# Mamba-2 scan and squared-ReLU feed-forward: halved first weight tiles, another load order, two small products on VectorE, and other idle products

## The chip, the cores and the metric

The kernel runs on one core of a Trainium2 chip. The metric is the device time of one execution in microseconds (us); lower is better. One execution of the kernel before was also recorded by the hardware profiler; times inside an execution are counted from the start of its span. Engines are called PE (TensorE), DVE (VectorE), ACT (ScalarE), POOL (GpSimd) and SP (SyncE, which here only issues transfers).

## The reference

Two stages follow each other. The first is a chunked state-space scan over x (4 batches, 8 heads, 768 positions, 32 wide), with a decay a per position and B and C (16 wide):

```python
for c in range(nc):                       # chunks along the sequence
    cum = np.cumsum(la, axis=-1)          # la = log(clip(a))
    L = np.exp(cum[..., :, None] - cum[..., None, :]) * causal
    M = np.einsum('bhin,bhjn->bhij', Cc, Bc) * L
    y = np.einsum('bhij,bhjd->bhid', M, xc) \
        + np.einsum('bhin,bhnd->bhid', Cc, state) * np.exp(cum)[..., None]
    state = decay_full[:, :, None, None] * state + np.sum(Bx, axis=2)
```

The second takes the result as 3072 tokens of 256 features:

```python
h = np.maximum(x @ w_in, 0.0)             # w_in 256 x 2048
out = h * h @ w_out                       # w_out 2048 x 256
```

## The kernel before, in words

The work is cut into 12 units of 256 positions: 4 batches times 3 stretches of the sequence, in the order batch first. A unit of the scan goes through these steps:

- loads of C, B and x (`ph_load`, L125; the third unit's x by `load_x`, L142);
- `prep_c`, `prep_b`, `prep_x` (L162 to L191): C times the running decay and B times its inverse are written as bf16 into the tile jt, two instructions each, and x is cast;
- `ph_tr` (L200): jt is transposed, by PE and copies for the first five units and by a transposing transfer for the rest, into bct;
- `ph_mt` (L244): sixteen small products give the raw scores in four PSUM banks; `ph_raw` (L261) copies a bank to SBUF by ACT, and `ph_mask` (L266) applies the causal mask on DVE, from PSUM or from such a copy, into mts;
- `ph_yu` (L273): the products that give the unit's outputs (from mts and from the carried state) and its contribution U to the state; the outputs are cast into the tile T;
- `ph_s` (L346): the new state z, and its bf16 spread S_d = z times QP, computed by POOL (`on_pool`, L366).

The feed-forward part works on T in steps of 256 hidden features, eight per unit: `mm1` (L381) makes four PE products with w_in and one ReLU by ACT into hb; `square` (L393) multiplies hb by itself on DVE into h; `mm2` (L399) makes four PE products with w_out. The weights are loaded by POOL's queue with a cast to bf16, w_in and w_out as four tiles of 512 hidden features each (`load_w_in`, L150, and `load_w_out`, L154).

Everything stands in an order written out by hand: a long opening sequence (L423 to L509) for the first two units, then the string `first`, in which u, s and d with two digits mean mm1, square and mm2 of a unit (first digit) and a step (second digit), and names such as `C2`, `B2`, `tr2` mean the third unit's scan steps; then a loop over the remaining steps. Each engine runs its instructions in this order, and each waits only for what it needs. In the opening sequence PE also runs products on a zero tile, `idle_products` (L157), whose numbers and widths stand in `NIDLE` (L50). POOL's queue carries, in the order of the program text, both POOL's arithmetic and its issues of weight loads, so that a load is issued only after the arithmetic ahead of it:

```python
        first = """
            u00 u01 s00 Y1 d00 s01 u10 z1b d01 u11 C2 s10 u02 s11 u03 d10 inv s02 u12 d11 s03 u13 d02 s12 d03 u04
            s13 d12 u05 B2 s04 d13 free tr2 load3 u14 s05 u15 d04 s14 mt2 d05 m20 s15 U2 m21 d14 m22 prep3 d15 u06 m23
            u16 lend s06 u07 s16 Y2 d06 u17 s07 d16 d07 s17""".split()
```

Of the kernel before, what the change touches and what calls it, by code (L numbers as in the profile page):

```python
# [11 lines left out]
BF16 = mybir.dt.bfloat16  # L12
# [18 lines left out]
def kernel(  # L31
# [13 lines left out]
    nc = tc.nc  # L45
# [1 line left out]
    NU = 12  # L47
    LAG = 4
    NPE = 5
    NIDLE = ((7, 512), (2, 256), (1, 256), (3, 256), (3, 128), (5, 256))  # L50

    const = ctx.enter_context(tc.tile_pool(name="const", bufs=1))
    wpool = ctx.enter_context(tc.tile_pool(name="w", bufs=1))
# [39 lines left out]
    idle = const.tile([128, 128], BF16, name="idle")  # L93


    w_in_b = [wpool.tile([128, 2, 512], BF16, name=f"w_in_b{i}") for i in range(4)]
    w_out_b = [wpool.tile([128, 4, 256], BF16, name=f"w_out_b{i}") for i in range(4)]
    QP = const.tile([128, 12, 2, 4], FP32, name="QP")

    pp = psum.tile([128, 8, 512], FP32, name="pp")  # L100
# [47 lines left out]
        live.setdefault(k, {})["xs"] = xs  # L148

    def load_w_in(i):  # L150
        nc.gpsimd.dma_start(  # L151
            out=w_in_b[i], in_=_dap(moe_w_in, i * 512, [[2048, 128], [128 * 2048, 2], [1, 512]]))

    def load_w_out(i):  # L154
        nc.gpsimd.dma_start(out=w_out_b[i], in_=_dap(moe_w_out, i * 512 * 256, [[1024, 128], [1, 1024]]))

    def idle_products(n, cols):  # L157
        for _ in range(n):
            nc.tensor.matmul(pp[:, 5, 0:cols], idle, _fap(idle, 0, [[0, cols // 128], [1, 128]]),  # L159
                             start=True, stop=True, skip_group_check=True)  # L160
# [39 lines left out]
    def ph_tr(k):  # L200
        v = live.setdefault(k, {})
        bct = big.tile([128, 2, 3, 128], BF16, tag="bct", name=f"bct{k}")
        v["bct"] = bct
        if k >= NPE:
            nc.sync.dma_start_transpose(out=bct.rearrange("p r w t -> p (r w) t"),
                                        in_=jt[k % 3].rearrange("p r w t -> p (r w t)"))
            return
        if k == 0:
            for r in range(2):
                tr = pp[:, 6 + r, 0:192].bitcast(BF16)  # L210
                for w in range(3):
                    nc.tensor.transpose(tr[:, w * 128:(w + 1) * 128], jt[0][:, r, w, :], eye_b)  # L212
                o = bct[:, r].rearrange("p w t -> p (w t)")
                if r == 0:
                    nc.vector.tensor_copy(out=o, in_=tr)
                else:
                    nc.scalar.copy(out=o, in_=tr)
            return
        if k == 1:
            for c, h in ((1, 7), (0, 6)):  # L220
                n = 1 + c
                tr = pp[:, h, 0:128 * n].bitcast(BF16)
                for r in range(2):
                    for w in range(n):
                        o = (r * n + w) * 128
                        nc.tensor.transpose(tr[:, o:o + 128], jt[1][:, r, c + w, :], eye_b)
                nc.scalar.copy(out=_fap(bct, 128 * c, [[384, 2], [1, 128 * n]]), in_=tr)
                if c:
                    idle_products(*NIDLE[4])
            return  # L230
        tr = pp[:, {2: 1, 3: 2}.get(k) or bank(), 0:384].bitcast(BF16)
        for r in range(2):
            for w in range(3):
                o = (r * 3 + w) * 128
                nc.tensor.transpose(tr[:, o:o + 128], jt[k % 3][:, r, w, :], eye_b)  # L235
        o = bct.rearrange("p r w t -> p (r w t)")
        if k == 4:
            nc.scalar.copy(out=o, in_=tr)
        else:
            nc.vector.tensor_copy(out=o, in_=tr)  # L240
# [102 lines left out]
            nc.scalar.copy(out=_fap(T[y], 0, [[64, 2], [128, 4], [1, 64]]),  # L343
                           in_=_fap(pp, h[0] * 512, [[(h[1] - h[0]) * 512, 2], [64, 4], [1, 64]]))

    def ph_s(k, i, later=None, raw=None):  # L346

        b, j = UNITS[k]
        v = live[k]
        if i == 0:  # L350
            v["S"] = [state.get(b, (None, None, None))[2]]
        if j == 2 and i == 1:
            return
        z_old, p_old, _ = state.get(b, (None, None, None))
        h, c = v["U"][i]
        held.discard(h)
        z = spool.tile([128, 64], FP32, tag=f"z{b}", name=f"z{k}_{i}")
        u_in = pp[:, h, c:c + 64] if raw is None else raw
        if z_old is None:
            nc.scalar.copy(out=z, in_=pp[:, h, c:c + 64])  # L360
        else:
            nc.vector.scalar_tensor_tensor(out=z, in0=z_old, scalar=p_old, in1=u_in,  # L362
                                           op0=ALU.mult, op1=ALU.add)
        S_d = spool.tile([128, 256], BF16, tag=f"Sd{b}{i}", name=f"Sd{k}_{i}")

        def on_pool():  # L366
            nc.gpsimd.tensor_tensor(  # L367
                out=_fap(S_d, 0, [[128, 2], [32, 4], [1, 32]]),
                in0=_fap(z, 0, [[32, 2], [0, 4], [1, 32]]),
                in1=_fap(QP, ((b * 3 + j) * 2 + i) * 4, [[0, 2], [1, 4], [0, 32]]), op=ALU.mult)  # L370

        if later is None:
            on_pool()
        else:
            later.append(on_pool)
        state[b] = (z, Ptot[:, i, b * 3 + j:b * 3 + j + 1], S_d)
        v["S"].append(S_d)
# [2 lines left out]

    def mm1(blk, fp, edge):  # L381
        h = bank(edge)
        wb, wo = fp // 2, 2 * (fp % 2)
        for i in range(2):
            for g in range(2):
                nc.tensor.matmul(pp[:, h, i * 256:(i + 1) * 256], _fap(w_in_b[wb], g * 512 + wo + i, [[4, 128]]),  # L386
                                 T[blk][:, g].rearrange("p r u t -> p (r u t)"),
                                 start=(g == 0), stop=(g == 1), skip_group_check=True)
# [9 lines left out]

    def mm2(blk, fp):  # L399
        h2 = h2s.pop((blk, fp))  # L400
        wb, wo = fp // 2, 2 * (fp % 2)
        end = blk == NU - 1
        for r, i in [(r, i) for r in range(2) for i in range(2)] if end else [(r, i) for i in range(2) for r in range(2)]:
            f = 2 * fp + i
            o = pp[:, r, 0:256] if end else pp[:, 7 if blk else 6, r * 256:(r + 1) * 256]
            nc.tensor.matmul(o, h2[:, i, r * 128:(r + 1) * 128], w_out_b[wb][:, wo + i, :],  # L406
                             start=(f == 0 and (end or r == 0)), stop=(f == 15), skip_group_check=True)
        if fp < 7:
            return
# [12 lines left out]
    with tc.manual_schedule():  # L422
# [25 lines left out]
        keep(quad, [[-32, 4]], 0, 1)  # L448
        keep(quad, [[32, 4]], 31, -1)
        idle_products(*NIDLE[0])  # L450
        nc.vector.tensor_scalar(out=a_cl, in0=a_nat, scalar1=1e-6, scalar2=1.0, op0=ALU.max, op1=ALU.min)
        for u in range(2):
            nc.vector.tensor_tensor_scan(out=cp_r[:, u * 128:(u + 1) * 128], data0=a_cl[:, u * 128:(u + 1) * 128],
# [53 lines left out]
        load_w_in(3)  # L507
        load_w_out(3)
        order[:] = [4, 5]  # L509

        def late_states():
# [24 lines left out]
        def scores_only():  # L536
            order[:] = [h for h in order if h > 3]

        phases = {
            "z1b": lambda: (ph_s(1, 1, later=later), ph_s(0, 1, later=later, raw=U01)), "Y1": second_outputs, "C2": lambda: prep_c(2, nc.gpsimd), "free": scores_only,  # L540
            "inv": lambda: nc.vector.reciprocal(out=_fap(Pinv, 1, [[96, 2], [3, 32], [1, 2]]),
                                                in_=_fap(P_sb, 1, [[96, 2], [3, 32], [1, 2]])),
            "B2": lambda: prep_b(2, nc.vector), "load3": later_loads, "lend": lambda: order.__setitem__(slice(None), [2, 3, 4, 5]),
# [2 lines left out]
        for q in range(4):  # L546
# [1 line left out]


        first = """  # L550
            u00 u01 s00 Y1 d00 s01 u10 z1b d01 u11 C2 s10 u02 s11 u03 d10 inv s02 u12 d11 s03 u13 d02 s12 d03 u04
            s13 d12 u05 B2 s04 d13 free tr2 load3 u14 s05 u15 d04 s14 mt2 d05 m20 s15 U2 m21 d14 m22 prep3 d15 u06 m23
# [91 lines left out]
```

## Time and profile before

| | before |
|---|---|
| median of 6 runs | 115.78 us (115.55 to 116.37) |
| the profiled execution: its own time | 115.55 us |
| the profiled execution: span from first to last instruction | 113.8 us |
| PE busy | 108.3 us, 95% of the span |
| DVE busy | 81.3 us, 71% |
| ACT busy | 74.9 us, 66% |
| POOL busy | 50.0 us, 44% |
| moved by DMA | 13.18 MB, mean 116 GB/s |

A row of the profile's timeline gives the start, the duration, the engine, the line of the kernel, the operation, the tiles it writes and reads, and how many instructions are merged into the row. In the chain of work that ended last, each piece is what released the next one; its start and length are in us. Landings are counted from the issue of a transfer to its last byte in place. Matmuls overlap, so the distance between two starts tells more of PE's pace than the duration of one.

### The profile page before, as it was taken

To read this page: it belongs to the slowest core of one execution; us is meant where nothing else is said; L and a number is where in the kernel's file an instruction comes from. 1 tells how busy PE (TensorE), PEld (TensorE's weight loads), DVE (VectorE), ACT (ScalarE), POOL (GpSimd) and SP (SyncE) were. 2 spreads that over 40 slices of the span, in tenths; PEclk is the share of its full clock that TensorE was granted. 3 is DMA by queue.
4 is the path that set the end of the run, shared out by engine and by line. 5 is a ranking of instruction groups with operands and counts; after the bars stand their busy time and mean duration, and the time that the engine had idled before them with its cause. 6 is when DMAs were issued, how large, how long until landed. Compare 5 with 4: busy or idle time off the path is not lost.

```text
span 113.8 us, 3913 instructions
## 1 busy us (share of the span) xinstructions
PE 108.3 (95%) x1599; PEld 93.3 (82%) x1599; DVE 81.3 (71%) x183; ACT 74.9 (66%) x138; POOL 50.0 (44%) x101
## 2 busy tenths in 40 slices
PE   6899799999999999999999999999999999999980
PEld 2266599978888989989989989889899899899960
DVE  4479869598798999859769777677578488354440
ACT  3345856638786686676777776767766767867830
POOL 6399598128988486471679056065020020000000
PEclk9999999999999999999999999999999999999999
DMA  3999999989891785939999996432042020110202
GB/s 70 205 167 164 153 215 140 163 143 197 128 264 57 124 204 108 169 98 116 197 226 122 129 139 112 100 116 51 0 124 46 9 91 3 61 37 0 92 0 92
DMA packets 44850, 13.18 MB, mean 116 GB/s; under 512 B 41376, under 2 KB 42848, under 8 KB 44832
## 3 DMA queue, kind: packets, MB, share of 16 engines
q1 hardware_dynamic: 40736, 10.13, 48.4%
q0 software_dynamic: 2800, 2.49, 14.6%
q10 hardware_dynamic: 1296, 0.32, 1.3%
q8 instruction: 12, 0.20, 0.8%
q14 instruction: 6, 0.05, 0.1%
HBM read 10.64 MB, written 3.15 MB: 121 GB/s over the span
## 4 chain that ended last, share of the span: by engine, by line
PE 91%; DVE 3%; ACT 2%; issue 1%
PE pp L386 38%; PE pp L406 37%; PE pp L283 7%; PE pp L250 4%; PE pp L159 3%; DVE mts L268 2%; PE pp L235 1%; ACT hb L390 1%; PE pp L212 1%; ACT T L343 1%; PE pp L460 1%; ACT jt L176 0%; DVE jt L178 0%; ACT osb L415 0%; PE pp L471 0%
## 5 line engine op out<-in xcount | busy, mean ns | idle before, releaser
L390 ACT ACTIVATE hb<-pp 128x512 bf16<-128x512 f32 x96 | 56.5, 597 | 25.2 <-PE pp L386 23.6
L386 PE MATMUL pp<-T,w_in_b 128*128 128x256 bf16 x384 | 56.6, 273 | 0.5 <-ACT T L343 0.5
L406 PE MATMUL pp<-w_out_b,h 128*128 128x256 bf16 x384 | 56.5, 273 | 0.0
L396 DVE TENSOR_TENSOR h<-hb 128x512 bf16<-128x512 bf16 x96 | 42.9, 453 | 18.7 <-ACT hb L390 18.5
L386 PEld LDWEIGHTS <-w_in_b 128*128 128x128 bf16 x384 | 41.3, 114 | 3.6 <-issue 2.4
L406 PEld LDWEIGHTS <-h 128*128 128x128 bf16 x384 | 37.2, 98 | 4.0 <-DVE h L396 0.4
L268 DVE TENSOR_TENSOR mts<-pp,mask 128x512 bf16<-128x512 f32 x45 | 30.4, 682 | 1.0 <-PE pp L250 0.8
L367 POOL TENSOR_TENSOR Sd<-z,QP 128x256 bf16<-128x256 f32 x20 | 12.6, 640 | 28.4 <-DVE z L362 25.1
L165 POOL TENSOR_TENSOR jt<-C_nat,P_sb 128x128 bf16<-128x128 f32 x22 | 10.6, 503 | 6.7 <-DMA C_nat<-in_C_dram 5.7
L178 POOL TENSOR_TENSOR jt<-B_nat,Pinv 128x128 bf16<-128x128 f32 x18 | 8.7, 504 | 0.5 <-PE pp L283 0.2
L362 DVE SCALAR_TENSOR_TENSOR z<-z,Ptot,pp 128x64 f32<-128x64 f32 x14 | 3.9, 280 | 5.3 <-ACT T L343 4.4
L343 ACT CAST T<-pp 128x512 bf16<-128x512 f32 x10 | 5.8, 585 | 2.5 <-PE pp L283 1.9
L190 POOL CAST xs<-x_nat 128x512 bf16<-128x512 f32 x10 | 7.1, 713 | 0.6 <-DMA x_nat<-in_x_dram 0.3
L159 PE MATMUL pp<-idle 128*128 128x256 bf16 (+2 forms) x21 | 6.3, 438 | 1.1 <-DVE idle L435 1.1
L419 ACT COPY osb<-pp 128x512 f32<-128x512 f32 x11 | 6.4, 582 | 0.2 <-PE pp L406 0.2
L283 PE MATMUL pp<-mts,xs 64*32 64x128 bf16 x352 | 5.4, 219 | 0.1
L250 PE MATMUL pp<-bct 32*64 32x256 bf16 x192 | 5.3, 291 | 0.0
L159 PEld LDWEIGHTS <-idle 128*128 128x128 bf16 x21 | 2.6, 140 | 2.6 <-issue 1.4
L283 PEld LDWEIGHTS <-xs 64*32 64x32 bf16 x352 | 3.6, 90 | 0.8 <-issue 0.7
L283 PE MATMUL pp<-bct,Sd 128*128 128x128 bf16 x40 | 4.2, 220 | 0.0
L283 PEld LDWEIGHTS <-Sd 128*128 128x128 bf16 x40 | 3.1, 98 | 0.5 <-POOL Sd L367 0.2
L151 POOL DMA_DIRECT2D w_in_b<-in_moe_w_in_dram x4 | 3.1, 784 | 0.3 <-issue 0.3
(67 smaller groups left out, 44.5 us busy)
## 6 DMA issues: line engine op xcount, KB each, us to landing
x_nat<-in_x_dram SPq DMA_DIRECT2D x11, 256.0 KB, 4.0
out_dram<-osb SPq DMA_DIRECT2D x11, 256.0 KB, 3.5
C_nat<-in_C_dram SPq DMA_DIRECT2D x11, 128.0 KB, 3.8
B_nat<-in_B_dram SPq DMA_DIRECT2D x9, 128.0 KB, 3.7
w_in_b<-in_moe_w_in_dram POOLq DMA_DIRECT2D x4, 256.0 KB, 6.4
w_out_b<-in_moe_w_out_dram POOLq DMA_DIRECT2D x4, 256.0 KB, 5.8
B_nat<-in_B_dram ACTq DMA_DIRECT2D x1, 128.0 KB, 3.3
C_nat<-in_C_dram POOLq DMA_DIRECT2D x1, 128.0 KB, 4.5
```

What stands on the lines that cost most here:

```text
L159: nc.tensor.matmul(pp[:, 5, 0:cols], idle, _fap(idle, 0, [[0, cols // 128], [1, 128]]), start=True, stop=True, skip_group_check=True)
L165: eng.tensor_tensor(out=_fap(jt[k % 3], 128 + 144 * g, [[384, 2], [32, 4], [1, 16]]), in0=_fap(loaded[k]["C"], 128 * g, [[16, 2], [32, 4], ...
L178: eng.tensor_tensor(out=o, in0=i, in1=_fap(Pinv, b * 24 + 12 * g + j, [[96, 2], [3, 4], [0, 16]]), op=ALU.mult)
L190: eng.tensor_copy(out=xs, in_=loaded[k]["x"])
L250: nc.tensor.matmul(pp[64 * u:64 * u + 64, q, r * 256:r * 256 + 256], bct[32 * q:32 * q + 32, r, 0, u * 64:u * 64 + 64], _fap(bct[32 * q:32 ...
L268: nc.vector.tensor_tensor(out=live[k]["mts"][:, q], in0=(pp[:, q, :] if t is None else t).rearrange("p (r g i) -> p r g i", r=2, g=2), in1 ...
L283: nc.tensor.matmul(dst, w, v, start=bool(need), stop=False, skip_group_check=True, **({} if pos is None else {"tile_position": pos}))
L367: nc.gpsimd.tensor_tensor(out=_fap(S_d, 0, [[128, 2], [32, 4], [1, 32]]), in0=_fap(z, 0, [[32, 2], [0, 4], [1, 32]]), in1=_fap(QP, ((b * 3 ...
L386: nc.tensor.matmul(pp[:, h, i * 256:(i + 1) * 256], _fap(w_in_b[wb], g * 512 + wo + i, [[4, 128]]), T[blk][:, g].rearrange("p r u t -> p ( ...
L390: nc.scalar.activation(out=hb.rearrange("p i t -> p (i t)"), in_=pp[:, h, :], func=AF.Relu)
L396: nc.vector.tensor_tensor(out=h2, in0=hb, in1=hb, op=ALU.mult)
L406: nc.tensor.matmul(o, h2[:, i, r * 128:(r + 1) * 128], w_out_b[wb][:, wo + i, :], start=(f == 0 and (end or r == 0)), stop=(f == 15), skip ...
```

## The change

The w_in and w_out tiles, four of 512 hidden features before, become five: two of 256 and three of 512, and each is loaded as a whole. The opening sequence loads the first two w_in tiles where it loaded the first w_in and w_out, and the two small w_out tiles later, ahead of the next w_in. One w_out tile is issued ahead of the third unit's C and B instead of behind them. The spread of the first unit's state and the third unit's `prep_c` go from POOL to DVE, the latter to a later place in `first`, directly ahead of `B2`. The second unit's third scores bank is copied by ACT before it is masked, and ACT's first such copy stands ahead of T. The list of idle products gets other numbers and a seventh entry.

```diff
-    NIDLE = ((7, 512), (2, 256), (1, 256), (3, 256), (3, 128), (5, 256))
+    NIDLE = ((7, 512), (2, 128), (4, 256), (2, 256), (4, 256), (3, 128), (3, 256))
...
+    W_TILES = [(0, 2), (256, 2), (512, 4), (1024, 4), (1536, 4)]
+    w_in_b = [wpool.tile([128, 2, 128 * n], BF16, name=f"w_in_b{f}") for f, n in W_TILES]
+    w_out_b = [wpool.tile([128, n, 256], BF16, name=f"w_out_b{f}") for f, n in W_TILES]
+    w_slice = [(i, n, f) for i, (_, n) in enumerate(W_TILES) for f in range(n)]
...
-    def ph_s(k, i, later=None, raw=None):
+    def ph_s(k, i, later=None, raw=None, eng=None):
...
-            nc.gpsimd.tensor_tensor(
+            (eng or nc.gpsimd).tensor_tensor(
...
         idle_products(*NIDLE[0])
+        idle_products(*NIDLE[1])
...
         load_w_in(0)
-        load_w_out(0)
-        idle_products(*NIDLE[1])
+        load_w_in(1)
+        idle_products(*NIDLE[2])
...
         prep_c(1, nc.gpsimd)
-        load_w_in(1)
-        idle_products(*NIDLE[2])
+        load_w_out(0)
+        load_w_out(1)
+        load_w_in(2)
+        idle_products(*NIDLE[3])
...
-        ph_s(0, 0)
+        prep_b(1, nc.vector)
+        ph_s(0, 0, eng=nc.vector)
         ph_raw(0, 2)
-        prep_b(1, nc.vector)
         prep_x(1, nc.gpsimd)
-        load_w_out(1)
-        load_w_in(2)
-        idle_products(*NIDLE[3])
+        load_w_out(2)
+        load_w_in(3)
+        idle_products(*NIDLE[4])
         ph_tr(1)
-        idle_products(*NIDLE[5])
+        idle_products(*NIDLE[6])
...
         ph_mt(1)
+        ph_raw(1, 3)
         ph_yu(y=0, late=True, h=(4, 5))
-        ph_raw(1, 3)
-        for q in range(4):
+        ph_raw(1, 2)
+        for q in (0, 1, 3, 2):
             ph_mask(1, q)
         ph_yu(u=1)
         ph_s(1, 0)
+        load_w_out(3)
         ph_load(2, "CB", nc.gpsimd)
-        load_w_out(2)
         load_x(2)
-        load_w_in(3)
-        load_w_out(3)
+        load_w_in(4)
+        load_w_out(4)
...
-        "C2": lambda: prep_c(2, nc.gpsimd)
+        "C2": lambda: prep_c(2, nc.vector)
...
-            u00 u01 s00 Y1 d00 s01 u10 z1b d01 u11 C2 s10 u02 s11 u03 d10 inv s02 u12 d11 s03 u13 d02 s12 d03 u04
-            s13 d12 u05 B2 s04 d13 free tr2 load3 ...
+            u00 u01 s00 Y1 d00 s01 u10 z1b d01 u11 s10 u02 s11 u03 d10 inv s02 u12 d11 s03 u13 d02 s12 d03 u04
+            s13 d12 u05 C2 B2 s04 d13 free tr2 load3 ...
```

More of the change, by code (lines that the diff above doesn't have):

```diff
@@ L93 @@
     idle = const.tile([128, 128], BF16, name="idle")
-    w_in_b = [wpool.tile([128, 2, 512], BF16, name=f"w_in_b{i}") for i in range(4)]
-    w_out_b = [wpool.tile([128, 4, 256], BF16, name=f"w_out_b{i}") for i in range(4)]
+    W_TILES = [(0, 2), (256, 2), (512, 4), (1024, 4), (1536, 4)]
+    w_in_b = [wpool.tile([128, 2, 128 * n], BF16, name=f"w_in_b{f}") for f, n in W_TILES]
+    w_out_b = [wpool.tile([128, n, 256], BF16, name=f"w_out_b{f}") for f, n in W_TILES]
+    w_slice = [(i, n, f) for i, (_, n) in enumerate(W_TILES) for f in range(n)]
     QP = const.tile([128, 12, 2, 4], FP32, name="QP")
@@ L150, in load_w_in @@
     def load_w_in(i):
-        nc.gpsimd.dma_start(
-            out=w_in_b[i], in_=_dap(moe_w_in, i * 512, [[2048, 128], [128 * 2048, 2], [1, 512]]))
+        f, n = W_TILES[i]
+        nc.gpsimd.dma_start(out=w_in_b[i], in_=_dap(moe_w_in, f, [[2048, 128], [128 * 2048, 2], [1, 128 * n]]))
     def load_w_out(i):
-        nc.gpsimd.dma_start(out=w_out_b[i], in_=_dap(moe_w_out, i * 512 * 256, [[1024, 128], [1, 1024]]))
+        f, n = W_TILES[i]
+        nc.gpsimd.dma_start(out=w_out_b[i], in_=_dap(moe_w_out, f * 256, [[256 * n, 128], [1, 256 * n]]))
     def idle_products(n, cols):
@@ L228, in ph_tr @@
                 if c:
-                    idle_products(*NIDLE[4])
+                    idle_products(*NIDLE[5])
             return
@@ L382, in mm1 @@
         h = bank(edge)
-        wb, wo = fp // 2, 2 * (fp % 2)
         for i in range(2):
+            wb, n, f = w_slice[2 * fp + i]
             for g in range(2):
-                nc.tensor.matmul(pp[:, h, i * 256:(i + 1) * 256], _fap(w_in_b[wb], g * 512 + wo + i, [[4, 128]]),
+                nc.tensor.matmul(pp[:, h, i * 256:(i + 1) * 256], _fap(w_in_b[wb], g * 128 * n + f, [[n, 128]]),
                                  T[blk][:, g].rearrange("p r u t -> p (r u t)"),
@@ L400, in mm2 @@
         h2 = h2s.pop((blk, fp))
-        wb, wo = fp // 2, 2 * (fp % 2)
         end = blk == NU - 1
@@ L404, in mm2 @@
             f = 2 * fp + i
+            wb, _, wf = w_slice[f]
             o = pp[:, r, 0:256] if end else pp[:, 7 if blk else 6, r * 256:(r + 1) * 256]
-            nc.tensor.matmul(o, h2[:, i, r * 128:(r + 1) * 128], w_out_b[wb][:, wo + i, :],
+            nc.tensor.matmul(o, h2[:, i, r * 128:(r + 1) * 128], w_out_b[wb][:, wf, :],
                              start=(f == 0 and (end or r == 0)), stop=(f == 15), skip_group_check=True)
@@ L539 @@
         phases = {
-            "z1b": lambda: (ph_s(1, 1, later=later), ph_s(0, 1, later=later, raw=U01)), "Y1": second_outputs, "C2": lambda: prep_c(2, nc.gpsimd), "free": scores_only,
+            "z1b": lambda: (ph_s(1, 1, later=later), ph_s(0, 1, later=later, raw=U01)), "Y1": second_outputs, "C2": lambda: prep_c(2, nc.vector), "free": scores_only,
             "inv": lambda: nc.vector.reciprocal(out=_fap(Pinv, 1, [[96, 2], [3, 32], [1, 2]]),
@@ L550 @@
         first = """
-            u00 u01 s00 Y1 d00 s01 u10 z1b d01 u11 C2 s10 u02 s11 u03 d10 inv s02 u12 d11 s03 u13 d02 s12 d03 u04
-            s13 d12 u05 B2 s04 d13 free tr2 load3 u14 s05 u15 d04 s14 mt2 d05 m20 s15 U2 m21 d14 m22 prep3 d15 u06 m23
+            u00 u01 s00 Y1 d00 s01 u10 z1b d01 u11 s10 u02 s11 u03 d10 inv s02 u12 d11 s03 u13 d02 s12 d03 u04
+            s13 d12 u05 C2 B2 s04 d13 free tr2 load3 u14 s05 u15 d04 s14 mt2 d05 m20 s15 U2 m21 d14 m22 prep3 d15 u06 m23
             u16 lend s06 u07 s16 Y2 d06 u17 s07 d16 d07 s17""".split()
```

## The prediction

> **What bounds the kernel now.** I read the page first: busy shares, granted clock, the chain's shares.
>
> ```profile
> PE 108.3 (95%) x1599; PEld 93.3 (82%) x1599; DVE 81.3 (71%) x183; ACT 74.9 (66%) x138; POOL 50.0 (44%) x101
> PEclk9999999999999999999999999999999999999999
> PE 91%; DVE 3%; ACT 2%; issue 1%
> ```
>
> TensorE (PE) is busy 95% and carries 91% of the chain that ended last. The change removes no product of the result, so it can gain only where PE waits or runs slowly. The chain in order of time, up to 36 us, shows where that is:
>
> ```profile
> 1.06 3.17 PE pp L159 x7
> ...
> 5.73 0.82 PE pp L212 x6
> ...
> 7.12 0.74 PE pp L250 x14
> ...
> 7.88 0.69 DVE mts L268
> 8.57 0.40 DVE jt L178 x2
> 8.97 1.95 DVE mts L268 x3
> ...
> 10.97 0.64 PE pp L283 x32
> ...
> 12.27 0.61 PE pp L386 x4
> ...
> 15.56 1.31 PE pp L386 x12
> ...
> 21.23 0.33 PE pp L235 x6
> ```
>
> Two things are to be seen. From 14 us on, the chain is PE alone: twelve 256-column products in 1.31 us, 109 ns each, without holes. All before that is a head in which ACT, DVE and PE hand one small job to the next. A head shorter by t ends the kernel t sooner, if no load comes late after it. And the head runs on slow products: seven 512-column ones take 3.17 us. Individual starts in the trace stand 427 ns apart, 0.83 ns a column, against 0.43 later. The pace doubles at 9.65 us, inside the last idle products. PEclk says 9 in all slices, so the starts are what to read here.
>
> Then the DVE and POOL timelines, for the 1.95 us of masks and for the loads, and the page's last part for landings:
>
> ```profile
> 9.49 1.08 DVE L268 TENSOR_TENSOR mts<-raw,mask 128x512 bf16<-128x512 bf16 x1
> 12.74 0.43 DVE L268 TENSOR_TENSOR mts<-raw,mask 128x512 bf16<-128x512 bf16 x1
> 9.68 0.61 POOL L190 CAST xs<-x_nat 128x512 bf16<-128x512 f32 x1
> 14.53 0.90 POOL L136 DMA_DIRECT2D B_nat<-in_B_dram  x1
> 19.62 0.48 DVE L178 TENSOR_TENSOR jt<-B_nat,Pinv 128x128 bf16<-128x128 f32 x2
> ...
> w_in_b<-in_moe_w_in_dram POOLq DMA_DIRECT2D x4, 256.0 KB, 6.4
> w_out_b<-in_moe_w_out_dram POOLq DMA_DIRECT2D x4, 256.0 KB, 5.8
> C_nat<-in_C_dram POOLq DMA_DIRECT2D x1, 128.0 KB, 4.5
> B_nat<-in_B_dram POOLq DMA_DIRECT2D x1, 128.0 KB, 4.1
> ```
>
> The same raw mask costs 0.43 us alone and 1.08 us beside POOL's Sd and cast of x (9.11 to 10.29). The third B lands at 14.53 + 4.1 = 18.63 and is used at 19.62: 1.0 us of slack. Landings follow each other, by issue time plus delay: w_in 11.29, w_out 12.49, w_in 14.73, w_out 16.13, w_in 17.53, C 18.09, B 18.63, w_out 20.40. That queue is a stream, and its order matters.
>
> **The change part by part**, against the profiled 115.55 us (span 113.8, 1.75 around it); the median of the six runs, 115.78, is 0.23 above.
>
> *Idle products.* Two 128-column ones follow the first seven (4.02 to 4.23, where PE waited for the scans) and two more 256-column ones fill 5.15 to 5.57, before jt is ready at 5.67: both free. One more ahead of L250 ends at 7.16 at slow pace where L250 began at 7.11: 0.05. One more ahead of the second unit's transposes costs 0.1, off the path: the masks end later than these. Two fewer stand at the end. What they may buy is an earlier doubling. Row: the pace doubled at 9.65. Rule (the Trainium skill, "TensorE: Matmul & The Clock Gate", "What's actually happening"): idle PE runs at half rate, and one busy free-running window of some 3.4 us releases it. Windows that end at 9.65 began at 6.24 and, before that, at 2.83; the 2.83 to 6.24 one has holes at 4.02 and 5.15, about 0.9 us, and just these are filled. By the row alone nothing comes earlier: 0. By the rule the doubling comes at 6.24, or for any phase by about 7.9: L250's stage (0.74 us; a later one of sixteen, 10.24 to 10.66, takes 0.42) shrinks by 0.3, the transposes before it by 0.1: 0.4. I take 0.4, since the holes named are closed, and keep 0.
>
> *First state to VectorE.* DVE gains one product of 128x256 between jt and the second mask. No such DVE row exists; L178 takes 0.20 a piece at half the elements, so about 0.33 (bounds 0.2, and POOL's own 0.62), on the path. It waits for z (ACT, ends 8.70) and QP (POOL, about 7.8), both in before its turn at 8.97; queued behind it are all the other masks. POOL loses Sd, and issues three loads (two w_out halves at 0.57, w_in at 0.76) ahead of the cast, so the cast starts about 10.5, not 9.68. The first raw mask then takes 0.43, not 1.08: -0.65. Net -0.3. In the second unit, one more raw copy on ACT makes one DVE mask cheaper (0.43 for 0.62), 0.2 off masks that the first outputs do not wait for; of the two copies one fits into the 1.47 us that ACT is idle before T, the other lies behind T beside the first w_in products. Its worst is the cast meeting a raw mask after all: +0.3.
>
> So the head is worth 0.3 + 0.4 = 0.7 at best: first w_in product at 11.6, not 12.27.
>
> *Halves.* Two w_in halves by 5.79 and 6.69; the first is in before 11.3, when the whole one came: no wait. The w_out halves are issued at 8.56 and 9.15 (whole: 6.69), behind QP and C of the second unit on POOL. First used about 13.3; landing estimated 12.9 to 13.3: just hidden. The next w_in goes out at 9.75, not 8.33. Packets in the trace last 98 ns for 1024 written bytes, 173 for 2048; on that line 512 cost 60. Per engine the halves add 2x16x60 - 16x98 = 0.35 us and 2x8x98 - 8x173 = 0.18: the stream is 0.5 us longer. That w_in lands about 15.1 (14.73 + 0.5, less a hole in the old stream about 13 us), and its product is due at 15.8 - 0.7 = 15.1. A wait of 0 to 0.4, which the next item hides.
>
> *Third w_out ahead of third C and B; third C to DVE.* C and B move behind one 256 KB tile (1.4 us between landings) and 0.5 of halves: B at 18.63 + 1.9 = 20.5, less up to 0.5 for the hole: 20.3. For the price of a load the rule and the rows part. Rule (the Trainium skill, "DMA: Bandwidth & Descriptors", "Anatomy of one DMA"): about 2.0 us and bytes at 436 GB/s, so 2.3 for B; issued at 14.85 it would be in at 17.2, never waited for. Rows: 4.1 to 4.5 in a queue that is never empty. I go by the rows; the rule gives the uncovered 0.7. On DVE, C (0.48, as L178) may start when C is in, about 19.75, then B (0.48) at 20.3, done 20.8; the transposes L235, at 21.07 now, come at 20.85, where a head shorter by 0.7 had them at 20.4. Queued behind on DVE is the square s04 (20.59 now, 20.8 then), whose product is due at 21.7: covered. Behind on PE is everything, in order. POOL loses C's 1.2 us, and nothing waits for that. The third w_out, in at 20.40 for a product at 22.28, was not late: coming earlier gains 0. Load 3 is released by the third unit's bct and moves with it.
>
> **Sum**: 0.7 of head, 0.45 given back at B: -0.25, so 115.3. The wait for B also swallows the scatter of the head, so I take no second figure for the median.
>
> **The rivals.**
> - *Uncovered:* B lands by 19.85 (the old stream's hole closes, the halves cost nothing). All 0.7 stays: 114.85. For it: three loads stand in the queue by 10.5, so the DMA engines need not run dry. Against: each extra packet is certain.
> - *The clock stays:* doubling at 9.65 or later. Only the 0.3 of the masks: B hides it nearly, 115.3 to 115.75. For it: the present run is at slow pace for 8.6 us though the first 3.2 were full.
> - *B too late, slower:* each us of B past 20.5 is paid one to one, since PE waits in order behind L235 and afterwards has no holes to win it back. It decides at a landing of 20.5, only 0.2 past my estimate. The stream ran thin for a us about 13 (100 to 120 KB a us by its packets, 180 to 200 elsewhere); if that comes on top of the longer stream, B lands at 21.3: +0.8, 116.35. The same end comes if the second w_in, issued 1.4 later, lands 1.4 later: 16.1 against 15.8. Against it: the engines were busy, so landings follow the bytes rather than the issue.
>
> **How the numbers follow.** Likeliest, B limits a shortened head: 0.40, 115.0 to 115.7. Uncovered: 0.13. Clock stays: 0.17. B too late: 0.30. A measurement of this kernel tells about 0.3%, 0.35 us, from no change: faster is under 115.43, slower over 116.13. The likeliest case gives 0.32 faster and 0.08 same; uncovered 0.13 faster; clock stays 0.03, 0.12, 0.02; too late 0.02 same, 0.28 slower. Together 0.48, 0.22, 0.30. The range is from the uncovered case to somewhat past the late one, 114.8 to 116.5. Of cases of both signs, the likeliest one's own range is the one named.
>
> **What would show it.** Right: products of 128 columns 53 ns apart before 8 us; the first raw mask at 0.43; the first w_in product about 11.6; an idle DVE ended by the DMA of C or B about 19.7 to 20.3; L235 at 20.85. Wrong: slow pace up to 9.65 again; L235 with no wait on B before it (then the gain is whole); a PE wait ended by a w_in or w_out landing before 20 us; or L235 after 21.1, and the kernel slower by what exceeds that.

## The result, and the profile after

| | before | after |
|---|---|---|
| median | 116.02 us (39 runs, 115.48 to 116.72) | 116.64 us (18 runs, 115.98 to 117.41) |
| ratio | | 1.0065 [1.0046, 1.0083] |
| the profiled execution, its time and span | 115.55, 113.8 us | 116.44, 114.7 us |

The change makes the kernel 0.65% slower; I had forecast 115.3 us and a small gain. The runs of before were made anew beside those of after, so the ratio is the number to use; it leaves out runs over 1.5% above the fastest of their kernel, and it is not the quotient of the two medians. The page of after:

```profile
PE 107.5 (94%) x1603; PEld 91.6 (80%) x1603; DVE 82.0 (71%) x186; ACT 75.4 (66%) x139; POOL 49.3 (43%) x100
PE 78%; DMA 9%; DVE 4%; SPq 2%; POOL 2%; ACT 1%; issue 1%; POOLq 0%
```

PE is busy for 0.8 us less and the span is 0.9 longer: PE waits more. The chain that ended last, 91% PE before, has 9% DMA in it now. In order of time (start, length, what):

```profile
3.67 4.49 DMA B_nat<-in_B_dram
...
8.40 0.28 DVE jt L181
8.68 0.34 DVE Sd L370
9.02 3.21 DVE mts L271 x5
...
13.74 0.55 POOL w_out_b L158
14.29 0.89 POOL C_nat L138
15.18 6.22 DMA B_nat<-in_B_dram
21.42 0.50 DVE jt L181 x2
21.97 0.51 PE pp L238 x6
```

Read it from the end. The third unit's transposes (L235 before, L238 here) start at 21.97 instead of 21.07, rows of before and of after:

```profile
21.07 0.50 PE L235 MATMUL pp<-eye_b,jt 128*128 128x128 bf16 x6
```

```profile
21.97 0.51 PE L238 MATMUL pp<-eye_b,jt 128*128 128x128 bf16 x6 [0.65 <-DVE jt L181]
```

They waited for DVE, DVE for B, and B came 6.22 us after its issue at 15.18, at 21.40. (Other landings below are an issue plus a delay that the profile gives to 0.1 us, so they are good to about 0.05.) The DVE timeline shows it as idle time with its releaser, and shows the head too:

```profile
7.35 0.69 DVE L271 TENSOR_TENSOR mts<-pp,mask 128x512 bf16<-128x512 f32 x1
8.19 0.49 DVE L181 TENSOR_TENSOR jt<-B_nat,Pinv 128x128 bf16<-128x128 f32 x2
8.60 0.42 DVE L370 TENSOR_TENSOR Sd<-z,QP 128x256 bf16<-128x256 f32 x1
8.93 0.68 DVE L271 TENSOR_TENSOR mts<-pp,mask 128x512 bf16<-128x512 f32 x1
9.54 1.49 DVE L271 TENSOR_TENSOR mts<-raw,mask 128x512 bf16<-128x512 bf16 x2
...
20.60 0.49 DVE L168 TENSOR_TENSOR jt<-C_nat,P_sb 128x128 bf16<-128x128 f32 x2 [0.80 <-DMA C_nat<-in_C_dram]
21.42 0.49 DVE L181 TENSOR_TENSOR jt<-B_nat,Pinv 128x128 bf16<-128x128 f32 x2 [0.33 <-DMA B_nat<-in_B_dram]
```

The first mask is 0.53 earlier than before (7.88), but the second starts at 8.93 where it was 8.89, and the first w_in product comes at 12.38, not 12.27. So of the 0.90 us at L238, 0.11 come from the head and the rest, 0.79, is the wait for B. Behind L238 the kernel keeps this distance to the end: 92.7 us from these transposes to the end of the span in both.

Why B is late stands in the DMA columns. POOL's queue is q0 (2800 packets before, 3216 after, by the halves' shorter lines). Two windows, 9 to 15 and 15 to 21 us (last columns: PEclk, DMA share, GB/s), of before, then of after with its queue line:

```profile
9.00:15.00 6.00, 5.29 (x130) 3.77 (x128) 5.54 (x12) 3.64 (x9) 4.62 (x8) 1.00 1.08 164
15.00:21.00 6.00, 6.00 (x58) 5.70 (x56) 4.27 (x11) 4.13 (x8) 4.37 (x7) 1.00 1.15 163
```

```profile
q0 software_dynamic: 3216, 2.49, 16.3%
...
9.00:15.00 6.00, 4.42 (x120) 2.71 (x118) 5.28 (x13) 3.60 (x9) 4.89 (x8) 1.00 0.89 126
15.00:21.00 6.00, 6.00 (x57) 5.65 (x56) 3.75 (x11) 4.04 (x8) 3.27 (x5) 1.00 1.64 199
```

From 9 to 15 the transfers moved 6 x (164 - 126) = 228 KB less than before; a whole weight tile is 256 KB as it is written. The first large w_in tile (hidden features 512 to 1023, the second w_in tile of before) shows it, issued at 9.26 and in at 15.66: 6.4 us. Everything queued behind it is late: w_out 16.89, w_in 18.24, third w_out 19.70, C 20.58, B 21.40.

### The profile page after: what moved, and what is told of

The parts are those of the page before. It is cut to its first block, busy times and chain, and to the rows that moved or that the text cites. A ratio compares the mean times of both kernels' runs of the same rounds, so it can differ in the third digit from the quotient of the medians.

```text
span 114.7 us, 3925 instructions
## 1 busy us (share of the span) xinstructions
PE 107.5 (94%) x1603; PEld 91.6 (80%) x1603; DVE 82.0 (71%) x186; ACT 75.4 (66%) x139; POOL 49.3 (43%) x100
## 3 DMA queue, kind: packets, MB, share of 16 engines
q0 software_dynamic: 3216, 2.49, 16.3%
## 4 chain that ended last, share of the span: by engine, by line
PE 78%; DMA 9%; DVE 4%; SPq 2%; POOL 2%; ACT 1%; issue 1%; POOLq 0%
PE pp L389 34%; PE pp L409 34%; DMA B_nat<-in_B_dram 9%; PE pp L286 6%; PE pp L253 3%; DVE mts L271 3%; SPq L138 2%; PE pp L238 1%; POOL C_nat L138 1%; DVE jt L181 1%; POOL Sd L370 1%; ACT raw L266 1%; POOL w_out_b L158 0%; SPq L426 0%; ACT osb L418 0%
## 5 line engine op out<-in xcount | busy, mean ns | idle before, releaser
L389 PEld LDWEIGHTS <-w_in_b 128*128 128x128 bf16 x384 | 40.1, 110 | 4.4 <-issue 2.4
L271 DVE TENSOR_TENSOR mts<-pp,mask 128x512 bf16<-128x512 f32 x44 | 29.8, 682 | 0.4 <-PE pp L253 0.2
L370 POOL TENSOR_TENSOR Sd<-z,QP 128x256 bf16<-128x256 f32 x19 | 11.9, 637 | 28.6 <-DVE z L365 25.5
L168 POOL TENSOR_TENSOR jt<-C_nat,P_sb 128x128 bf16<-128x128 f32 x20 | 9.2, 478 | 6.2 <-DMA C_nat<-in_C_dram 6.2
L162 PE MATMUL pp<-idle 128*128 128x256 bf16 (+2 forms) x25 | 5.7, 366 | 1.1 <-DVE idle L438 1.1
L154 POOL DMA_DIRECT2D w_in_b<-in_moe_w_in_dram x5 | 3.8, 767 | 0.3 <-issue 0.3
```

The costliest lines, as they stand in the source:

```text
L168: eng.tensor_tensor(out=_fap(jt[k % 3], 128 + 144 * g, [[384, 2], [32, 4], [1, 16]]), in0=_fap(loaded[k]["C"], 128 * g, [[16, 2], [32, 4], ...
L271: nc.vector.tensor_tensor(out=live[k]["mts"][:, q], in0=(pp[:, q, :] if t is None else t).rearrange("p (r g i) -> p r g i", r=2, g=2), in1 ...
L370: (eng or nc.gpsimd).tensor_tensor(out=_fap(S_d, 0, [[128, 2], [32, 4], [1, 32]]), in0=_fap(z, 0, [[32, 2], [0, 4], [1, 32]]), in1=_fap(QP ...
```

## The experiments

Theories at the start: **(a)** B's wait is the loss, made by one tile ahead of it and by a stream that the halves thin; **(b)** the head is the loss, since S_d went onto DVE's path and the raw masks did not get cheaper; **(c)** the new idle products cost or bring nothing. Ratios are to before. I give the place of a load by what POOL issues it behind.

**1. Order and tile size.**

e1, the changed kernel with C and B ahead of the third w_out again:

```diff
-        load_w_out(3)
         ph_load(2, "CB", nc.gpsimd)
+        load_w_out(3)
```

> The changed kernel with one line moved back: C and B of the third unit are issued ahead of the third w_out again. Theory (late B): the kernel after lost 0.9 us because the third B landed at 21.38 and the transposes of the third unit waited 0.81 us for it. With B ahead of the 256 KB of w_out it lands about 1.5 us sooner, near 19.9, is masked by nothing, and the transposes start at 21.1 to 21.2 with no wait: the kernel is within 0.2 us of the kernel before (ratio 0.999 to 1.003). Rival (VectorE): the loss is the new work on VectorE (Sd and the third C), and the order of the loads only shows where it ends; then the time stays about 0.6% over the kernel before.

Measured: 116.28 us, 1.0007 [0.9984, 1.0029]. B landed at 19.66 and nothing waited for it. So the wait was worth 0.6% of time, all of the loss; but the 0.7 of head that the prediction counted on isn't there either: the first w_in product comes at 12.38 as in after. (Part 3 shows why.) Its profile (116.78) shows another cost, rows of PE of after and of e1:

```profile
12.38 1.03 PE L389 MATMUL pp<-T,w_in_b 128*128 128x256 bf16 x8 [0.49 <-ACT T L346]
```

```profile
12.38 1.86 PE L389 MATMUL pp<-T,w_in_b 128*128 128x256 bf16 x8 [0.49 <-ACT T L346]
```

The same eight products from the same start take 1.86 us: PE went back to half pace until about 15.6 (granted clock 0.50 from 12.2 to 15.6), and the twelve products that begin at 15.49 in after begin at 16.57. This is not what e1's median is made of. The stretch lowers the mean granted clock of the profiled execution to 0.983, and only four of the 22 runs of e1 stand below 0.99; the other eighteen have a median of 115.97, still within 0.1 us of before (116.08).

e2, the kernel before with its third w_out ahead of C and B:

```diff
+        load_w_out(2)
         ph_load(2, "CB", nc.gpsimd)
-        load_w_out(2)
```

> The kernel before with the third w_out issued ahead of the third C and B and nothing else. Theory (late B is the sum of several delays): B moves from 18.63 to about 20.0 here; it is used at 19.62 now, so its product on VectorE ends near 20.5 instead of 20.1, and the transposes at 21.07 still do not wait: no difference (within 0.2 us). So the order alone is not enough and the longer stream of the halves is needed as well. Rival (the order alone): B lands at 21 or later, and the kernel loses 0.4 us or more.

Measured: 115.73 us, 0.9962 [0.9946, 0.9979]: faster, which no theory had. B landed at 20.11 and the transposes did not wait. What its profile gained lies in the head: the first w_in product comes at 12.10 instead of 12.27, with PE at full pace by 4.75 instead of 9.65. The edit comes behind both, so why the median is lower stays open. With the stream of before, the order is no harm.

e3, the changed kernel with four whole tiles in the places of before, third w_out still first:

```diff
-    W_TILES = [(0, 2), (256, 2), (512, 4), (1024, 4), (1536, 4)]
+    W_TILES = [(0, 4), (512, 4), (1024, 4), (1536, 4)]
...
         load_w_in(0)
-        load_w_in(1)
+        load_w_out(0)
...
-        load_w_out(0)
-        load_w_out(1)
-        load_w_in(2)
+        load_w_in(1)
```

> The changed kernel with four whole tiles of w_in and of w_out, issued in the places that the kernel before has for the first two of them; the third w_out stays ahead of C and B. Theory (halves lengthen the stream): B lands 0.5 to 1.3 us sooner than in the kernel after (21.38), at 20.1 to 20.9, the wait of the third transposes falls from 0.81 to 0 to 0.4 us, and the kernel is at the level of the one before or up to 0.4 us over. Rival (order alone): B lands at 21.2 or later, and the loss of 0.6% stays.

Measured: 115.48 us, 0.9952 [0.9934, 0.9969]. B landed at 20.98 in a profiled execution of 116.18, the longest of its runs. e5 is e3 with C and B first:

> The changed kernel with whole tiles and with C and B of the third unit ahead of the third w_out: the fourth corner beside after (halves, w_out first: +0.65%), the one with C and B first (halves: +0.07%) and the one with whole tiles (w_out first: -0.48%). Theory (the halves make the load stream late, and only the later C and B feel the order): with whole tiles the order decides little, since B is in time either way: within 0.2 us of the whole tiles with w_out first, that is 0.3 to 0.6% faster than the kernel before. Rival (w_out first is a gain of its own with whole tiles, as the kernel before gained 0.4% from it): 0.3 to 0.5 us slower than the whole tiles with w_out first, level with the kernel before.

Measured: 115.41 us, 0.9942 [0.9921, 0.9962], B at 18.48. With whole tiles the order costs nothing that can be told (0.9952 and 0.9942), with halves 0.6% (1.0065 and 1.0007). And the change with whole tiles in the places of before is a gain of some 0.5%, hidden under the loss of the rest; e3 and e5 take back the size of the first tiles and the place of the first w_out together, and part 3 separates them. e8 makes the check from the other side, the kernel before with only the halves:

> The kernel before with the halves alone: w_in and w_out tiles cut as in the kernel after and issued in its places, C and B ahead of the third w_out, all else as before. Theory (halves deepen the thin stretch of the stream and put the second w_in off): the third C, made by POOL here behind all issues, and B land about 1 us later than now (19.1 and 19.6), which VectorE's and POOL's slack of 1 us just covers; the second w_in lands near 15.6 with its product due at 15.8: 0 to 0.5 us slower than the kernel before. Rival (halves help as they let the first product start sooner): 0.2 us or more faster.

Measured: 116.19 us, 1.0009 [0.999, 1.0027], the first large w_in in at 16.05, C and B at 19.58 and 19.93: the stream is thin there as well (125 GB/s from 9 to 15), and with C and B ahead of the third w_out it costs nothing that can be told.

**2. Head and idle products.**

e4, the kernel before with the idle products of after (`NIDLE` and one call more, as in the change):

> The kernel before with the idle products of the kernel after and nothing else. Theory (clock): the pace of PE doubles before 6.3 us instead of at 9.65, the first mask starts near 7.35 instead of 7.88, but the second unit's B lands only about 8.1 and the raw masks still run beside POOL's cast, so of 0.5 us some 0.2 are left at the first w_in product: 0.1 to 0.3 us faster. Rival (no use): the pace doubles at the same time, or all of it is taken by the masks: no difference.

Measured: 116.06 us, 1.0006 [0.9986, 1.0026]. The pace doubled early (by 4.75), but in this profile the first w_in landed at 12.74 and the second at 16.76, both waited for; the chain of e4:

```profile
8.36 8.38 DMA w_in_b<-in_moe_w_in_dram
16.78 1.07 PE pp L386 x8
```

This load was issued at 8.36, as in before (8.33), and landed 2 us later than there, and the first w_in 1.4 later; why is not known. So this run can't tell what the idle products earn where the loads allow it. e13 does it again with whole tiles, e5 with the idle products of before:

> Whole tiles with C and B ahead of w_out (0.9942), and the idle products of the kernel before. If the refill makes PE's pace double earlier, as my step on idle products had it, this kernel loses up to 0.4 us: 0.996 to 0.998. If the refill is worth nothing, as its run on top of the kernel before showed (1.0006, but with two late weight loads in its profile), the ratio is 0.994 again.

Measured: 115.58 us, 0.9972 [0.9947, 0.9997], against 0.9942 [0.9921, 0.9962] with the refill. 0.3% between them, and the intervals overlap: the refill may earn what I had put (0.4 us) or nothing. Its profile doubled the pace by 4.88 with the holes open, as e2's did by 4.75; so closing the holes is not what an early doubling needs.

e6, the changed kernel with the second unit's S_d on DVE too, so that POOL issues the third w_out, C and B without a pause:

```diff
-        ph_s(1, 0)
+        ph_s(1, 0, eng=nc.vector)
         load_w_out(3)
```

> The changed kernel with the spread of the second unit's first state on VectorE too, so that POOL's queue does not stand still from 11.97 to 13.08 us and issues the third w_out, C and B 1.7 us sooner (C about 12.6, B about 13.5 instead of 15.18). Theory (the DMA engines set the landings: with the halves their rate falls to 70 to 80 KB a us between 11.5 and 14.5 us, where 180 to 200 are reached elsewhere): the loads ahead of B are no sooner done, B lands at 21.0 to 21.4 as before, and the time stays at 0.5 to 0.7% over the kernel before. Rival (the issue sets them: the thin stretch is the queue's own pause): the thin stretch ends about 12.5 to 13, B lands at 20 or sooner, and the time comes down by 0.6 us or more.

Measured: 116.83 us, 1.0057 [1.0029, 1.0085]. The chain of e6:

```profile
13.34 8.71 DMA B_nat<-in_B_dram
22.08 0.50 DVE jt L181 x2
```

B was issued 1.84 us earlier than in after and landed 0.7 later. For B the issue does not set the landing, the stream does.

e12, e5 with the first unit's S_d back on POOL (`ph_s(0, 0)`):

> Whole tiles, third C and B first, and the first unit's spread S_d back on POOL. If S_d on DVE is a cost of 0.33 us on the path that bought nothing, since the raw masks met the cast of x anyway, this kernel is 0.2 to 0.3 us faster than the same with S_d on DVE (0.9942): 0.991 to 0.993. If S_d on POOL makes the masks dear again (1.08 beside S_d and the cast, and a cast that comes 0.6 later), it is the same or up to 0.3 us slower: 0.994 to 0.997.

Measured: 115.73 us, 0.9976 [0.9958, 0.9994]; S_d on DVE is the better by 0.3 us (115.41), with intervals that just overlap. The raw masks of e12, then of e5:

```profile
9.14 1.56 DVE L271 TENSOR_TENSOR mts<-raw,mask 128x512 bf16<-128x512 bf16 x2
```

```profile
9.41 1.04 DVE L271 TENSOR_TENSOR mts<-raw,mask 128x512 bf16<-128x512 bf16 x2
```

S_d on DVE takes 0.33 us of its path and makes the pair 0.52 cheaper. e7, e3 with the second unit's cast of x moved from POOL to ACT:

```diff
-        prep_x(1, nc.gpsimd)
...
         ph_tr(1)
+        prep_x(1, nc.scalar)
```

> The changed kernel with whole tiles, and the second unit's x cast by ScalarE behind its two bct copies instead of by POOL. Theory (the raw masks are slowed by POOL's cast): both raw masks take 0.43 us instead of 0.74 to 0.82, the first outputs begin 0.6 us sooner, and the kernel is 0.2 to 0.5 us faster than the one with whole tiles alone (ratio 0.991 to 0.9935), as far as the first w_in tile, in at 11.3 to 11.9, lets it. Rival (the first w_in tile is the limit already): the masks are faster, the first w_in product starts no sooner, and the time stays within 0.1 us of the whole tiles alone (0.995).

Measured: 115.40 us, 0.9941 [0.9913, 0.997]: no better than e3 by the interval, though its first w_in product came at 11.58. The chain of e7 holds why: B's landing at 20.09 kept the transposes, by about 0.2 us. e11 is e7 with C and B first:

> Whole tiles, third C and B ahead of third w_out, and the cast of the second unit's x by ACT: the parts that the runs so far show to be good, together. Whole tiles with C and B first gave 0.9942; with the cast on ACT but w_out first 0.9941, where B still held the third unit's transposes for about 0.2 us. If that wait was all that hid the gain of the cast, the ratio is about 0.992 (115.1 to 115.2). If nothing is to be had any more (the first outputs are not what the end waits for), it is 0.994 again.

Measured: 114.99 us, 0.992 [0.9894, 0.9947]; the profiled execution 114.78. This is the fastest kernel of the study. Its median is 0.4 below those of e5 and e7, but from six runs, and the intervals of the ratios overlap. Its DVE rows:

```profile
9.32 0.75 DVE L271 TENSOR_TENSOR mts<-raw,mask 128x512 bf16<-128x512 bf16 x2
...
19.18 0.48 DVE L181 TENSOR_TENSOR jt<-B_nat,Pinv 128x128 bf16<-128x128 f32 x2
```

Two raw masks in 0.75, less than the 0.82 that one takes in after, and no idle time at B. POOL was issuing a weight load beside them (9.30 to 10.02), so here it is its arithmetic that makes a raw mask dear, not its issues.

**3. Is it the size of the halves or their place?** The change halves the tiles, and it also issues the first w_out 1.4 us later (8.13, not 6.69), behind the second unit's C. In e9 only w_in is in halves, in e10 only w_out, at the places of after. In both, the first 512 hidden features of h meet the rows of w_out in another order, so these two kernels compute something else and serve for timing alone; the products are the same in number and shape.

> The changed kernel with only w_in in halves: w_out comes as four whole tiles, the first of them where the two halves stood. With both in halves the time stood at 1.0065 of before, with none at 0.9952. If the w_in halves thin the stream, the written KB per half us stay at 40 to 60 from 11.5 to 15, the second large w_in lands about 15.7, B about 21.4, and the ratio is 1.003 to 1.007. If the w_out halves do it, the stream is full after 12.5 as in the kernel before, B lands by 20.6, and the ratio is 0.993 to 0.998.

Measured: 116.57 us, 1.0018 [0.9997, 1.004]; B at 21.19.

> The changed kernel with only w_out in halves: w_in comes as four whole tiles, the first of them where the two halves stood. If the w_in halves thin the stream, it is full here, B lands by 20.6 and the ratio is 0.993 to 0.998. If the w_out halves do it, the thin stretch of 11.5 to 15 stays, B lands about 21.4, and the ratio is 1.003 to 1.007. If each does half of it, this and the run with w_in halves alone both stand about 1.000 and each shows a thin stretch of half the length.

Measured: 116.66 us, 1.0061 [1.0034, 1.0088]; B at 21.84. Both have a slow stream (138 and 121 GB/s from 9 to 15), so whole w_out tiles alone did not cure it. e14 keeps the halves and puts them where before had its first w_out; e15 keeps whole tiles (as e3) and puts the first w_out where after has its halves:

```diff
 e14
         load_w_in(1)
+        load_w_out(0)
+        load_w_out(1)
...
-        load_w_out(0)
-        load_w_out(1)
         load_w_in(2)
```

```diff
 e15
         load_w_in(0)
-        load_w_out(0)
...
+        load_w_out(0)
         load_w_in(1)
```

> The changed kernel with its two w_out halves issued right behind the two w_in halves, where the kernel before issued its first w_out. Sizes as in the change, places as before. If the size thins the stream, the stretch of 11.5 to 15 at some 40 KB per half us stays, B lands about 21.2 and the ratio stays near 1.0065. If the late place does it, the stream runs at 75 to 100 KB there, B lands at 20.5 to 21 as with whole tiles, and the ratio is 0.995 to 0.998.

Measured: 116.96 us, 1.0062 [1.0024, 1.01].

> The changed kernel with whole tiles (0.9952 where w_out stood in its old place), but with the first w_out issued behind the second unit's C, where the change issues its halves. Places as in the change, sizes as before. If the place thins the stream, the thin stretch appears and the ratio is 1.002 to 1.007. If the size does it, the stream is full, B lands by 21, and the ratio stays at 0.994 to 0.997.

Measured: 116.33 us, 1.0008 [0.9981, 1.0036]. The window 9 to 15 us of e14, then of e15, and B's wait in e15:

```profile
9.00:15.00 6.00, 4.85 (x118) 2.93 (x118) 4.02 (x9) 3.62 (x8) 4.79 (x8) 0.71 1.11 157
```

```profile
9.00:15.00 6.00, 4.61 (x124) 3.04 (x123) 5.28 (x13) 3.97 (x10) 4.89 (x8) 1.00 0.86 119
```

```profile
21.53 0.49 DVE L181 TENSOR_TENSOR jt<-B_nat,Pinv 128x128 bf16<-128x128 f32 x2 [0.29 <-DMA B_nat<-in_B_dram]
```

All with the third w_out first:

| first tiles | first w_out | GB/s, 9 to 15 us | B landed | ratio |
|---|---|---|---|---|
| whole (e3) | old place | 157 | 20.98 | 0.9952 |
| whole (e15) | late place | 119 | 21.55 | 1.0008 |
| halves (e14) | old place | 157 | 20.91 | 1.0062 |
| halves (after) | late place | 126 | 21.40 | 1.0065 |

The place thins the stream, whatever the size. All 17 kernels of this case fall in line: the seven with the late place (after, e1, e6, e8, e9, e10, e15) moved 119 to 138 GB/s from 9 to 15, the ten with the old one 157 to 187. With whole tiles the place alone costs 0.56%.

The place costs the head too. POOL's cast of the second unit's x stands behind these issues. Rows of after, of e15 and of e5:

```profile
9.96 0.77 POOL L193 CAST xs<-x_nat 128x512 bf16<-128x512 f32 x1
```

```profile
9.74 0.86 POOL L193 CAST xs<-x_nat 128x512 bf16<-128x512 f32 x1
...
9.71 1.17 DVE L271 TENSOR_TENSOR mts<-raw,mask 128x512 bf16<-128x512 bf16 x2
...
12.23 1.03 PE L389 MATMUL pp<-T,w_in_b 128*128 128x256 bf16 x8 [0.49 <-ACT T L346]
```

```profile
9.24 0.60 POOL L193 CAST xs<-x_nat 128x512 bf16<-128x512 f32 x1 [0.45 <-DMA x_nat<-in_x_dram]
...
11.81 1.03 PE L389 MATMUL pp<-T,w_in_b 128*128 128x256 bf16 x8 [0.49 <-ACT T L346]
```

In after the cast ends at 10.73, the two raw masks at 11.03, and the first w_in product starts at 12.38. In all six late-place kernels with S_d on DVE (after, e1, e6, e9, e10, e15) the masks end 0.3 us behind the cast, and that product starts 1.63 to 1.65 us behind it: the end of the cast sets the head, at 12.23 to 12.38. In the six changed kernels with whole tiles in the old place the product starts at 11.42 to 12.06. So e1, which waits for no B, is still 0.57 us behind e5 at its first w_in product.

That e14 is still slow has another cause: the issues of four halves. Its profiled execution (118.46) ran at half pace from 12 to 16 (granted clock 0.50) and is the longest of its runs, so besides the stream I take only POOL's rows from it, and those of e3 beside them. The eight of its 14 runs with a granted clock above 0.99 have a median of 116.53, a us over e3, so the half pace is not the cause.

```profile
5.47 1.61 POOL L154 DMA_DIRECT2D w_in_b<-in_moe_w_in_dram  x2 [0.29 <-issue]
7.07 1.10 POOL L158 DMA_DIRECT2D w_out_b<-in_moe_w_out_dram  x2
8.18 0.40 POOL L479 TENSOR_TENSOR QP<-Ptot,quad 128x96 f32<-128x96 f32 x1
8.56 0.99 POOL L168 TENSOR_TENSOR jt<-C_nat,P_sb 128x128 bf16<-128x128 f32 x2
```

```profile
6.68 0.57 POOL L158 DMA_DIRECT2D w_out_b<-in_moe_w_out_dram  x1
7.26 0.37 POOL L477 TENSOR_TENSOR QP<-Ptot,quad 128x96 f32<-128x96 f32 x1
7.58 0.78 POOL L168 TENSOR_TENSOR jt<-C_nat,P_sb 128x128 bf16<-128x128 f32 x2
```

A half costs POOL as much to issue as a whole tile: 0.55 against 0.57 for w_out; for w_in the first issue takes 0.90 and a later one about 0.75, half or whole. Early in the queue the four halves push QP and the second unit's C back by a us, and with C the second unit's transposes (their first product waits 1.06 us for C in e14) and scores. Late in the queue they spare C, thin the stream and put off the cast. Whole tiles in the old place avoid all three.

In after's places the halves cost 1.0065 - 1.0008, 0.6%, over e15 (0.3 us by the medians), though both profiles look alike (spans 114.7 and 114.9). The half pace of e1 is not the reason, as every run's mean granted clock shows: 1.000 in the profile of after without such a stretch, 0.983 with one in e1, 0.971 with one twice as long in e14. Of the 19 executions of after with a clock on record five stand at 0.983 to 0.985; the other fourteen still have a median of 116.60. None of e15's 14 stands below 0.998; their median is 116.33. The difference goes with the halves of w_out, not with those of w_in: in the runs above 0.99 e10 has 116.59 and e9 116.14. What fits is the second w_out issue, 0.55 us more on POOL's queue ahead of the cast. From the start of QP to the end of the cast POOL takes 3.50 to 3.63 us with w_out in halves (after, e1, e6, e10), and 3.11 to 3.18 with it whole (e9, e15). No run moves the cast alone in these places, so this is argued and not shown.

Which kernels fall back to half pace is open. It is no mark of the halves: 17 of the 69 runs of before that were made beside e1, and 8 of the 22 of e9, stand below 0.99. None of the 70 runs of e3, e5, e7, e11 and e15 does.

## Why the prediction was wrong

Two terms of the sum failed: the landing of B (put at 20.3, measured 21.40), and the head (put at 0.7, measured -0.11). The first decides in the profile of after; the second shows in e1, which does not wait for B and is no faster than before.

- **Halves** is the step behind the first. I had the large w_in at 15.1 and the stream 0.5 us longer, from packet lengths. It was issued at 9.26, half a us earlier than I had put it, and landed at 15.66. The packets were not the term: with halves in the old place the stream keeps its 157 GB/s. What I passed over was the place, POOL's C and QP ahead of the w_out issues; I took the issue times into account but let "landings follow the bytes rather than the issue". For this tile they followed the issue: 0.93 us later than in before at both, 6.4 us apart in both. My figure for the thin us about 13, 100 to 120 KB, was also read too low: the windows of before give 131 GB/s from 12 to 13 and 151 from 13 to 14. The w_out halves themselves, put at 12.9 to 13.3, landed at 11.9 and 12.6 and were never waited for.
- **Third w_out ahead of third C and B**: the sum put B at 20.3 and decided at 20.5; it landed at 21.40. The price past that point was as said: 0.8 us of PE's wait, with nothing later that wins it back. The rival *B too late* (B at 21.3, +0.8) is what happened, 0.89 in the profiles; of its two reasons, the later issue of the large w_in is seen, and the longer packets do not show in the rate. The order is a cost only on a thinned stream: e5 against e3. My choice of the row over the rule of the Trainium skill ("DMA: Bandwidth & Descriptors", "Anatomy of one DMA") was right in direction: 2.3 us estimated by the rule, 4.1 to 4.5 by the rows, 6.22 measured.
- **First state to VectorE** is the step behind the second. S_d on DVE took 0.33 us, as put. The 0.65 from a raw mask that meets no cast did not come. The cast began at 9.96, not 10.5, since the issues ahead of it were earlier, and the masks ended 0.3 us behind its end: 1.49 for the two, as before (1.42). And part of the early first mask went into waiting for the second unit's B, whose product starts only at 8.19. With whole tiles in the old place the step is worth about the 0.3 I had (e12 against e5), and in e11, with the cast on ACT, the two raw masks take 0.75 together.
- **Idle products**: I took 0.4; the first mask came 0.53 earlier. That the refill did it is not shown: e2 and e13 doubled as early without it, the run of before that I read doubled late, and e13 can't tell 0.3% from nothing. The row that I read, 9.65, was one draw of something that varies from run to run.
- **C to VectorE** was costed at nothing beside B; DVE did take C while it waited for B. It was not tried alone.
- **The sum**: 0.7 of head was -0.11. The 0.5 to 0.6% that whole tiles in the old place give is about what I had forecast for the head, but in part by luck: e3 and e5 start their first w_in product 0.4 to 0.5 us earlier than before, not 0.7.

## What to carry to other kernels

Where one engine both computes and issues loads, a split tile can cost a full issue for each piece (0.55 against 0.57 us here), and the pieces stand either ahead of arithmetic that is on the path or behind it: count both before splitting, and ask what the engine's later work, here the cast, will then meet. Read the bytes moved per us in a window, not only the gaps between landings, when loads are moved in such a queue; the third B, behind a thin stretch, paid for it however early it was issued (e6). Undo a change part by part even when it lost: with the first tiles whole and in their old place the rest was a gain of 0.5% (e3), though not every part of that rest was tried alone.

## What the runs showed that I had not expected

- The late place of one 256 KB load (issued at 8.44 in e15, 6.68 in e3) cost the stream more than its own delay: 119 to 138 GB/s for 6 us against 157 to 187. Packets wait although their issue is done: in after, POOL had issued the next three tiles by 11.97, and the stream was thin until 15. Why was not found; it is not POOL's pause (e6).
- The end of POOL's cast of x set the first w_in product in six kernels: 1.63 to 1.65 us behind it in each.
- PE fell back to half pace in some runs, and in e1's profile stayed there for 3.4 us: 1.08 us lost.
- When PE's pace doubled varied between runs with the same idle products: at 9.65 us in before, by 4.75 in e2, by 4.88 in e13.
